# Agent attention and a tanh feed-forward: the low part of the hidden tile for two of eight pairs by DMA, and no f32 passes

## The chip, the core and the metric

One core of a Trainium2 chip. The metric is device time in microseconds of the whole program, inputs in HBM to output in HBM; three runs of the kernel before gave 2227.61, 2227.90 and 2228.77 us, median 2227.9.

## What is computed

Four batches of 12480 queries go through an attention with 49 agents in place of the keys, and the result through a feed-forward layer of width 2048 with the nonlinearity h - tanh(h):

```python
a2k = sm(agents, k)          # 49 x 12480, scale 1/sqrt(128)
agent_v = a2k @ v            # 49 x 128
q2a = sm(q, agents)          # 12480 x 49
x = q2a @ agent_v            # 12480 x 128, for each of 4 batches
h = x @ w_in                 # 128 -> 2048
g = h - np.tanh(h)
out = g @ w_out              # 2048 -> 128
```

## The kernel before

`agent_v @ w_in` is folded into one 49 x 2048 matrix per batch, kept as a high and a low part (`awh`, `awl`), so that h comes straight from the softmax weights of the queries. The program has a start (batch 0's keys and values, the weights, which arrive as 64-bit floats and are decoded), and then one long loop.

The loop runs over 104 blocks of 480 queries, and in each block over 8 **pairs** of hidden chunks (a chunk is 128 of the 2048 hidden units, so a pair tile is 128 partitions x 960 values). That makes 832 steps. One step of pair k, and the name of each piece, which the rest uses:

- **m1** (L398, L399, TensorE): four matmuls of 480 columns write h into PSUM. Three PSUM buffers hold h, so m1 of pair k+3 waits until pair k has been read.
- **y, z** (L408, L410, ScalarE): y = tanh(c h), z = y*y.
- **g** (L412, VectorE): g = h*z. The host-side factor makes this the small-h form of h - tanh(h).
- **gh** (L442, GpSimd): g rounded to the matmul's short f32 format (fp32r), the high part.
- **gl** (L447, VectorE): g - gh, the low part.
- **m2** (L459, L460, L461, TensorE): for each of the two chunks three matmuls of 480 columns into the block's accumulator: gh by the low and by the high part of w_out (`wo_l`, `wo_h`), and gl by `wo_h`. So six for a pair.

One pair in sixteen is **plain**: the last pair of every even block (`PLAIN_PAIR`, `PLAIN_EVERY`) has no gh and no gl; its g is multiplied in full f32 by `wo_f` (L457), which the hardware runs as two instructions for each chunk, four for the pair. There are 52 plain pairs and 780 others.

Beside the loop run, in pieces, the softmax of the queries two blocks ahead (L353 to L390) and, in batches 0 to 2, the next batch's keys and values (L228 to L290). Loads and stores are all issued by SyncE (SP): the queries `qt`, the keys `kt`, the values `v`, the output.

The order of the instructions on each engine is set by a scheduler when the program is built; `LAG1` and `LAG2` keep the gl and the m2 one step each behind in the text of the program. At run time each engine works through its own list in that order and waits where an operand or a free buffer is missing. The `NB` table gives the number of buffers of each tile.

Of the kernel before, what the change touches and what calls it, by code (L numbers as in the profile page):

```python
# [11 lines left out]
F32 = mybir.dt.float32  # L12
F32R = mybir.dt.float32r
# [4 lines left out]
AF = mybir.ActivationFunctionType  # L18
ALU = mybir.AluOpType
# [3 lines left out]
B, N, C = 4, 12480, 128  # L23
A = 49
A2 = 2 * A
FF = 2048
NCH = FF // 128
# [7 lines left out]
BLK = 480  # L35
# [21 lines left out]
T0 = 13  # L57
# [15 lines left out]
class Build:  # L73
# [11 lines left out]
        self.work = ctx.enter_context(self.pool(name, reuse_waits="tile"))  # L85

    def wtile(self, tag, bufs):
        return self.work.tile([128, 1024], F32, tag=tag, name=tag, bufs=bufs)

    def misc(self):  # L90
        return self.pmisc.tile([128, 512], F32, tag="misc", name="misc")
# [1 line left out]
    def constants(self):  # L93
        nc = self.nc
        c = self.const
        self.ag = c.tile([128, B, A], F32, tag="ag", name="ag")
        nc.sync.dma_start(self.ag, self.agT.rearrange("b c a -> c b a"))
        self.ident = c.tile([128, 128], F32, tag="ident", name="ident")
        make_identity(nc, self.ident)
        self.identr = c.tile([128, 128], F32R, tag="identr", name="identr")  # L100
        nc.vector.tensor_copy(self.identr, self.ident)
        self.ones = c.tile([128, 128], F32, tag="ones", name="ones")
        nc.vector.memset(self.ones, 1.0)
        self.mx = c.tile([128, NP * B], F32, tag="mx", name="mx")
# [4 lines left out]
        self.wo_f = c.tile([128, 2, C], F32, tag="wo_f", name="wo_f")  # L109
# [40 lines left out]

    def load_w_out(self, c, raw):
        nc = self.nc
        w = self.work.tile([128, 512], F32, tag="wf", name="wf", bufs=2)
        self.decode(raw, w)
        h = self.wo_h[:, 4 * c : 4 * c + 4, :].rearrange("p n e -> p (n e)")
        l = self.wo_l[:, 4 * c : 4 * c + 4, :].rearrange("p n e -> p (n e)")
        nc.scalar.copy(h, w)
        nc.vector.tensor_tensor(l, w, h.bitcast(F32), ALU.subtract)
        if c == PLAIN_PAIR // 2:
            nc.scalar.copy(self.wo_f.rearrange("p n e -> p (n e)"), w[:, 2 * C * (PLAIN_PAIR % 2) :][:, : 2 * C])  # L160

    def phase1(self, b):
        nc = self.nc
        st = {}
        kb, vb = (KV0 if b == 0 else KV), VB

# [125 lines left out]
        def sums():  # L292
            yield
            yield
            acc, an = (st["ps"] if b == 0 else st["acc"]), st["acc"]
            sm = self.small.tile([128, 1], F32, tag="sm", name="sm")
            nc.vector.tensor_scalar(sm[:A], acc[:A, C : C + 1], EPS, None, ALU.add)
            nc.vector.reciprocal(sm[:A], sm[:A])
            nc.vector.tensor_scalar(an[:A, :C], acc[:A, :C], sm[:A], None, ALU.mult)
            pt = self.misc()  # L300
            nc.tensor.transpose(pt[:, :A], an[:A, :C], self.ident[:A, :A])
# [103 lines left out]
    def act(self, h):  # L405
        nc = self.nc
        y = self.pair(self.wtile("y", NB["y"]))
        nc.scalar.activation(y, h[:, :, :BLK], AF.Tanh, scale=TSC)  # L408
        z = self.wtile("z", NB["z"])[:, : 2 * BLK]
        nc.scalar.activation(z, y.rearrange("p c n -> p (c n)"), AF.Square)  # L410
        g = self.wtile("g", NB["g"])[:, : 2 * BLK]
        nc.vector.tensor_tensor(self.pair(g), h[:, :, :BLK], self.pair(z), ALU.mult)  # L412
# [26 lines left out]

    def high(self, g):  # L440
        gh = self.wtile("gh", NB["gh"])[:, : 2 * BLK].bitcast(F32R)
        self.nc.gpsimd.tensor_scalar(gh, g, 1.0, 0.0, ALU.mult, ALU.add)  # L442
        return gh

    def low(self, g, gh):
        gl = self.wtile("gl", NB["gl"])[:, : 2 * BLK].bitcast(F32R)
        self.nc.vector.tensor_tensor(gl, g, gh.bitcast(F32), ALU.subtract)  # L447
        return gl

    def m2(self, acc, i, gh, gl):  # L450
        nc = self.nc
        for c in range(2):
            f = 2 * i + c
            x = slice(c * BLK, (c + 1) * BLK)
            first, last = f == 0, f == NCH - 1
            if gl is None:
                nc.tensor.matmul(acc[:, :BLK], self.wo_f[:, c, :], gh[:, x], start=first, stop=last)  # L457
# [3 lines left out]
            nc.tensor.matmul(acc[:, :BLK], self.wo_h[:, f, :], gl[:, x], start=False, stop=last)  # L461

    def fast(self):
        nc, tc = self.nc, self.tc
# [41 lines left out]
        rest0 = p1[2 * NG + 5 :] + [t_job(1)]  # L506
        live = []
        kq = []
        q1, q2, done = [], [], []
        acc, outs = {}, {}  # L510

        def start(gen):
# [18 lines left out]

        def rest(n, i, h):
            g = self.act(h)
            even = n % PLAIN_EVERY == 0
            plain = even and i == PLAIN_PAIR
            gh = None if plain else self.high(g)
            q1.append((n, i, g, gh))

        def low(keep):
            while len(q1) > keep:  # L540
                n, i, g, gh = q1.pop(0)
                q2.append((n, i, g, None) if gh is None else (n, i, gh, self.low(g, gh)))

        def out(keep):
            while len(q2) > keep:
                n, i, gh, gl = q2.pop(0)
                if i == 0:
                    acc[n] = self.misc()
                self.m2(acc[n], i, gh, gl)
                if i == HP - 1:  # L550
                    done.append(n)

        for n, i in steps:
            b = blocks[n][0]
            pos = (n % 2) * HP + i
            p = n // 2
            if n % NBLK == 0 and i == 0 and b + 1 < B:
                kq = self.phase1(b + 1)
            h = foreground(n, i)
# [84 lines left out]
```

## Time and profile before

| | |
|---|---|
| median of the runs | 2227.9 us |
| span of the profiled execution, first to last instruction | 2226.8 us |
| steps in the loop | 832 |
| TensorE busy | 2181.5 us |
| VectorE busy | 2044.3 us |
| ScalarE busy | 1812.7 us |
| GpSimd busy | 1410.9 us |
| moved by the SP queue | 106.68 MB |
| mean granted TensorE clock | 0.992 |

The times of single instructions come from this one execution, whose span is 1.1 us below the median of the runs. Matmuls overlap: one that is listed with 0.38 us can be followed by the next 0.22 us later, and so the time from start to start is what a matmul costs in a row of them, and the busy time says only that the engine had something under way.

### The profile page before, as it was taken

To read this page: it belongs to the slowest core of one execution; us is meant where nothing else is said; L and a number is where in the kernel's file an instruction comes from. 1 tells how busy PE (TensorE), PEld (TensorE's weight loads), DVE (VectorE), ACT (ScalarE), POOL (GpSimd) and SP (SyncE) were. 2 spreads that over 40 slices of the span, in tenths; PEclk is the share of its full clock that TensorE was granted. 3 is DMA by queue.
4 is the path that set the end of the run, shared out by engine and by line. 5 is a ranking of instruction groups with operands and counts; after the bars stand their busy time and mean duration, and the time that the engine had idled before them with its cause. 6 is when DMAs were issued, how large, how long until landed. Compare 5 with 4: busy or idle time off the path is not lost.

```text
span 2226.8 us, 31246 instructions
## 1 busy us (share of the span) xinstructions
PE 2181.5 (98%) x11083; PEld 1838.3 (83%) x11083; DVE 2044.3 (92%) x2107; ACT 1812.7 (81%) x2179; POOL 1410.9 (63%) x957
## 2 busy tenths in 40 slices
PE   7699999999999999999999999999999999999998
PEld 7588878888888887888888888788888888888887
DVE  6998998889998999888999999988999999999998
ACT  3478887778887877877888878877889989898987
POOL 2555566656765647665666555766666767676776
PEclk9899999999999999999999999999999999999999
DMA  9411111211011110211011210121010000000000
GB/s 300 120 56 56 57 37 47 65 50 35 28 46 56 56 58 30 63 56 58 19 36 38 65 55 21 37 64 49 19 36 19 28 27 28 27 27 27 27 10 20
DMA packets 76658, 108.75 MB, mean 49 GB/s; under 512 B 4048, under 2 KB 56528, under 8 KB 76496
## 3 DMA queue, kind: packets, MB, share of 16 engines
q1 hardware_dynamic: 76496, 106.68, 15.1%
q8 instruction: 91, 1.49, 0.3%
q14 instruction: 71, 0.58, 0.1%
HBM read 81.10 MB, written 25.56 MB: 48 GB/s over the span
## 4 chain that ended last, share of the span: by engine, by line
PE 90%; DVE 5%; POOL 2%; issue 1%; ACT 1%; DMA 0%; POOLq 0%; SPq 0%; ACTq 0%; DVEq 0%
PE h L398 16%; PE h L399 15%; PE misc L461 15%; PE misc L459 14%; PE misc L460 14%; PE misc L457 4%; PE misc L353 4%; PE misc L276 3%; PE misc L228 3%; DVE gl L447 1%; DVE g L412 1%; POOL gh L442 1%; PE h L209 1%; PE misc L385 1%; PE misc L327 0%
## 5 line engine op out<-in xcount | busy, mean ns | idle before, releaser
L442 POOL TENSOR_SCALAR gh<-g 128x960 fp32r<-128x960 f32 x780 | 1201.8, 1542 | 636.1 <-DVE g L412 488.9
L447 DVE TENSOR_TENSOR gl<-g,gh 128x960 fp32r<-128x960 f32 x780 | 977.6, 1254 | 88.6 <-PE misc L461 62.3
L412 DVE TENSOR_TENSOR g<-h,z 128x960 f32<-128x960 f32 x832 | 950.9, 1147 | 55.7 <-ACT z L410 53.3
L408 ACT ACTIVATE y<-h 128x960 f32<-128x960 f32 x832 | 804.2, 971 | 214.1 <-PE h L399 207.6
L410 ACT ACTIVATE z<-y 128x960 f32<-128x960 f32 x832 | 832.5, 1007 | 24.8 <-DVE g L412 7.8
L398 PE MATMUL h<-pT,awh 98*128 98x480 f32 x1664 | 666.9, 401 | 1.8 <-DVE g L412 1.3
L399 PE MATMUL h<-pT,awl 98*128 98x480 f32 x1664 | 631.6, 380 | 0.0
L461 PE MATMUL misc<-gl,wo_h 128*128 128x480 f32 x1560 | 608.7, 390 | 3.9 <-DVE gl L447 3.8
L459 PE MATMUL misc<-gh,wo_l 128*128 128x480 f32 x1560 | 594.2, 381 | 3.8 <-POOL gh L442 3.6
L460 PE MATMUL misc<-gh,wo_h 128*128 128x480 f32 x1560 | 591.2, 379 | 0.0
L398 PEld LDWEIGHTS h<-pT,awh 98*128 98x128 f32 x1664 | 312.8, 188 | 65.3 <-issue 14.0
L399 PEld LDWEIGHTS h<-pT,awl 98*128 98x128 f32 x1664 | 314.5, 189 | 58.8 <-issue 11.9
L461 PEld LDWEIGHTS misc<-gl,wo_h 128*128 128x128 f32 x1560 | 292.4, 187 | 59.1 <-DVE gl L447 8.7
L459 PEld LDWEIGHTS misc<-gh,wo_l 128*128 128x128 f32 x1560 | 294.3, 189 | 54.0 <-POOL gh L442 11.1
L460 PEld LDWEIGHTS misc<-gh,wo_h 128*128 128x128 f32 x1560 | 292.9, 188 | 47.9 <-issue 0.2
L378 POOL TENSOR_TENSOR pp<-qe,pp 120x392 fp32r<-120x392 f32 x52 | 70.6, 1357 | 67.9 <-ACT pp L376 67.6
L353 PEld LDWEIGHTS misc<-ag,qt 128*120 128x120 f32 x832 | 96.8, 187 | 3.3
L353 PE MATMUL misc<-ag,qt 128*120 128x49 f32 x832 | 94.2, 267 | 0.0
L457 PE MATMUL misc<-g,wo_f 128*128 128x480 f32 x208 | 92.6, 567 | 0.0
L366 POOL TENSOR_TENSOR qe<-qe,qm 120x392 f32<-120x392 f32 x52 | 71.0, 1366 | 30.0 <-ACT qe L364 29.9
L522 ACT ACTIVATE o<-misc 128x480 f32<-128x480 f32 x104 | 58.7, 565 | 36.4 <-PE misc L457 22.8
L276 PEld LDWEIGHTS misc<-v,ke 128*49 128x49 f32 (+1 forms) x588 | 62.0, 123 | 17.5 <-issue 12.9
(85 smaller groups left out, 993.7 us busy)
## 6 DMA issues: line engine op xcount, KB each, us to landing
qt<-qT SPq DMA_DIRECT2D x52, 480.0 KB, 3.4
outT<-o SPq DMA_DIRECT2D x52, 480.0 KB, 2.6
kt<-kT SPq DMA_DIRECT2D x48, 512.0 KB, 3.6
v<-v SPq DMA_DIRECT2D x48, 512.0 KB, 4.1
raw<-w_in SPq DMA_DIRECT2D x4, 512.0 KB, 7.8
raw<-w_out SPq DMA_DIRECT2D x4, 512.0 KB, 9.5
kt<-kT SPq DMA_DIRECT2D x4, 128.0 KB, 2.0
v<-v SPq DMA_DIRECT2D x4, 64.0 KB, 1.9
```

The source lines that it names most:

```text
L353: nc.tensor.matmul(ps[:TT, t * A : (t + 1) * A], qt[:, t * TT : (t + 1) * TT], self.ag[:, b, :], start=True, stop=True)
L398: nc.tensor.matmul(h[:, c, :BLK], aw[0][:A2, sl], pT[:A2], start=True, stop=False)
L399: nc.tensor.matmul(h[:, c, :BLK], aw[1][:A2, sl], pT[:A2], start=False, stop=True)
L408: nc.scalar.activation(y, h[:, :, :BLK], AF.Tanh, scale=TSC)
L410: nc.scalar.activation(z, y.rearrange("p c n -> p (c n)"), AF.Square)
L412: nc.vector.tensor_tensor(self.pair(g), h[:, :, :BLK], self.pair(z), ALU.mult)
L442: self.nc.gpsimd.tensor_scalar(gh, g, 1.0, 0.0, ALU.mult, ALU.add)
L447: self.nc.vector.tensor_tensor(gl, g, gh.bitcast(F32), ALU.subtract)
L457: nc.tensor.matmul(acc[:, :BLK], self.wo_f[:, c, :], gh[:, x], start=first, stop=last)
L459: nc.tensor.matmul(acc[:, :BLK], self.wo_l[:, f, :], gh[:, x], start=first, stop=False)
L460: nc.tensor.matmul(acc[:, :BLK], self.wo_h[:, f, :], gh[:, x], start=False, stop=False)
L461: nc.tensor.matmul(acc[:, :BLK], self.wo_h[:, f, :], gl[:, x], start=False, stop=last)
```

## The change

The f32 passes are gone: every pair has a gh, with `wo_f` replaced by a third copy of w_out. In two of the eight pairs of a block (i = 1 and i = 5; 208 in all) VectorE's gl is replaced by two DMAs: SP copies g into the gl tile (L455), and then a DMA on GpSimd's queue adds gh to it (L459). For the sum to be a difference, gh is made with the opposite sign of g. The signs are set by negating the folded matrix (`avs`), so that g comes out negated and gh positive, and gl is the negated low part, multiplied by the negated `wo_n`. In the text below such a pair is called a **late pair**: its four high matmuls (L468, L469) stand at its place in m2, and its two low ones (L471) behind the m2 of the next pair.

Buffers: gh 3 to 4, gl 2 to 3, the keys' tiles in the loop 3 to 2, the decode tile of w_out 2 to 1; the work tiles have 960 instead of 1024 columns.

```diff
-KV = 3
+KV = 2
-PLAIN_PAIR = NCH // 2 - 1
-PLAIN_EVERY = 2
+DMA_EVERY = 4
+DMA_AT = 1
-NB = dict(y=2, z=2, g=4, gh=3, gl=2)
+NB = dict(y=2, z=2, g=4, gh=4, gl=3)
...
-        w = self.work.tile([128, 512], F32, tag="wf", name="wf", bufs=2)
+        w = self.work.tile([128, 512], F32, tag="wf", name="wf", bufs=1)
...
-        if c == PLAIN_PAIR // 2:
-            nc.scalar.copy(self.wo_f.rearrange("p n e -> p (n e)"), w[:, 2 * C * (PLAIN_PAIR % 2) :][:, : 2 * C])
+        n = self.wo_n[:, 4 * c : 4 * c + 4, :].rearrange("p n e -> p (n e)")
+        nc.scalar.activation(n, h.bitcast(F32), AF.Copy, scale=-1.0)
...
-            nc.vector.tensor_copy(self.avs[:, b, :A], pt[:, :A])
-            nc.scalar.copy(self.avs[:, b, A:], pt[:, :A])
+            nc.vector.tensor_scalar(self.avs[:, b, :A], pt[:, :A], -1.0, None, ALU.mult)
+            nc.scalar.activation(self.avs[:, b, A:], pt[:, :A], AF.Copy, scale=-1.0)
...
-        self.nc.gpsimd.tensor_scalar(gh, g, 1.0, 0.0, ALU.mult, ALU.add)
+        self.nc.gpsimd.tensor_scalar(gh, g, -1.0, 0.0, ALU.mult, ALU.add)
...
-        self.nc.vector.tensor_tensor(gl, g, gh.bitcast(F32), ALU.subtract)
+        gl = self.low_tile()
+        self.nc.vector.tensor_tensor(gl, g, gh.bitcast(F32), ALU.add)
         return gl

-    def m2(self, acc, i, gh, gl):
+    def low_copied(self, g):
+        gl = self.low_tile()
+        self.nc.sync.dma_start(gl.bitcast(F32), g)
+        return gl
+
+    def low_added(self, gl, gh):
+        self.nc.gpsimd.dma_start(gl.bitcast(F32), gh.bitcast(F32), accum_op=ALU.add)
+        return gl
+
+    def m2(self, acc, i, gh, gl, high=True, low=True):
...
-            if gl is None:
-                nc.tensor.matmul(acc[:, :BLK], self.wo_f[:, c, :], gh[:, x], start=first, stop=last)
-                continue
-            nc.tensor.matmul(acc[:, :BLK], self.wo_l[:, f, :], gh[:, x], start=first, stop=False)
-            nc.tensor.matmul(acc[:, :BLK], self.wo_h[:, f, :], gh[:, x], start=False, stop=False)
-            nc.tensor.matmul(acc[:, :BLK], self.wo_h[:, f, :], gl[:, x], start=False, stop=last)
+            if high:
+                nc.tensor.matmul(acc[:, :BLK], self.wo_l[:, f, :], gh[:, x], start=f == 0, stop=False)
+                nc.tensor.matmul(acc[:, :BLK], self.wo_h[:, f, :], gh[:, x], start=False, stop=False)
+            if low:
+                nc.tensor.matmul(acc[:, :BLK], self.wo_n[:, f, :], gl[:, x], start=False, stop=f == NCH - 1)
...
-            gh = None if plain else self.high(g)
-            q1.append((n, i, g, gh))
+            gh = self.high(g)
+            q1.append((n, i, g, gh, self.low_copied(g) if i % DMA_EVERY == DMA_AT else None))
...
-                self.m2(acc[n], i, gh, gl)
+                self.m2(acc[n], i, gh, gl, low=not late)
+                while q3:
+                    self.m2(*q3.pop(0), high=False)
+                if late:
+                    q3.append((acc[n], i, gh, gl))
```

Three places in the order that the scheduler made.

On TensorE the plain pair is gone. Before, at the end of an even block (names carry the tile's buffer number; h is the result of m1, gh and gl are the operands of m2, misc is the accumulator):

```order
L461 MATMUL misc_20133<-gl_20258,wo_h_84 128x480
L457 MATMUL misc_20133<-g_20256,wo_f_86 128x480 x2
L398 MATMUL h_20333<-pT_20150,awh_15307 128x480
L399 MATMUL h_20333<-pT_20150,awl_15308 128x480
L398 MATMUL h_20333<-pT_20150,awh_15307 128x480
L399 MATMUL h_20333<-pT_20150,awl_15308 128x480
```

In the change every pair has its six rows, as the next excerpt shows for gl_19698. It is again TensorE, around the low matmuls of one late pair, whose high part is gh_19651 and whose low part is gl_19653:

```order
L468 MATMUL misc_19570<-gh_19651,wo_l_85 128x480
L469 MATMUL misc_19570<-gh_19651,wo_h_84 128x480
L398 MATMUL h_19756<-pT_19587,awh_15741 128x480
L399 MATMUL h_19756<-pT_19587,awl_15742 128x480
L398 MATMUL h_19756<-pT_19587,awh_15741 128x480
L399 MATMUL h_19756<-pT_19587,awl_15742 128x480
L468 MATMUL misc_19570<-gh_19675,wo_l_85 128x480
L469 MATMUL misc_19570<-gh_19675,wo_h_84 128x480
L471 MATMUL misc_19570<-gl_19698,wo_n_86 128x480
L468 MATMUL misc_19570<-gh_19675,wo_l_85 128x480
L469 MATMUL misc_19570<-gh_19675,wo_h_84 128x480
L471 MATMUL misc_19570<-gl_19698,wo_n_86 128x480
L471 MATMUL misc_19570<-gl_19653,wo_n_86 128x480 x2
```

The high matmuls of the late pair stand first, then m1 of the fifth pair after it (h_19756), then the whole m2 of the next pair, and only then the two low ones.

On GpSimd, two late pairs (gh_19651, and gh_19744, which comes four pairs later):

```order
L442 TENSOR_SCALAR gh_19651<-g_19649 128x960
L459 DMA gl_19653<-gh_19651 128x960
L366 TENSOR_TENSOR qe_19641<-qe_19641,qm_19640 120x392
L442 TENSOR_SCALAR gh_19675<-g_19673 128x960
L442 TENSOR_SCALAR gh_19696<-g_19694 128x960
L442 TENSOR_SCALAR gh_19719<-g_19717 128x960
L442 TENSOR_SCALAR gh_19744<-g_19742 128x960
L442 TENSOR_SCALAR gh_19770<-g_19768 128x960
L378 TENSOR_TENSOR pp_19736<-qe_19641,pp_19736 120x8x49
L459 DMA gl_19746<-gh_19744 128x960
```

The adding DMA stands right behind its gh, or, as for the second one and for most of the 208, behind the gh of the next pair.

More of the change, by code (lines that the diff above doesn't have):

```diff
@@ L87, in wtile @@
     def wtile(self, tag, bufs):
-        return self.work.tile([128, 1024], F32, tag=tag, name=tag, bufs=bufs)
+        return self.work.tile([128, 2 * BLK], F32, tag=tag, name=tag, bufs=bufs)
     def misc(self):
@@ L508, in fast @@
         kq = []
-        q1, q2, done = [], [], []
+        q1, q2, q3, done = [], [], [], []
         acc, outs = {}, {}
@@ L533, in rest @@
             g = self.act(h)
-            even = n % PLAIN_EVERY == 0
-            plain = even and i == PLAIN_PAIR
-            gh = None if plain else self.high(g)
-            q1.append((n, i, g, gh))
+            gh = self.high(g)
+            q1.append((n, i, g, gh, self.low_copied(g) if i % DMA_EVERY == DMA_AT else None))
         def low(keep):
             while len(q1) > keep:
-                n, i, g, gh = q1.pop(0)
-                q2.append((n, i, g, None) if gh is None else (n, i, gh, self.low(g, gh)))
+                n, i, g, gh, gl = q1.pop(0)
+                late = gl is not None
+                q2.append((n, i, gh, self.low_added(gl, gh) if late else self.low(g, gh), late))
         def out(keep):
             while len(q2) > keep:
-                n, i, gh, gl = q2.pop(0)
+                n, i, gh, gl, late = q2.pop(0)
                 if i == 0:
                     acc[n] = self.misc()
-                self.m2(acc[n], i, gh, gl)
+                self.m2(acc[n], i, gh, gl, low=not late)
[3 more added lines that the diff above has]
+                    q3.append((acc[n], i, gh, gl))
                 if i == HP - 1:
```

6 lines of the change are left out of this document (3 added, 3 removed).

## The prediction

> **What bounds the kernel now.** I read the page first: the busy times and the chain of work that ended last.
>
> ```profile
> span 2226.8 us, 31246 instructions
> PE 2181.5 (98%) x11083; PEld 1838.3 (83%) x11083; DVE 2044.3 (92%) x2107; ACT 1812.7 (81%) x2179; POOL 1410.9 (63%) x957
> PE 90%; DVE 5%; POOL 2%; issue 1%; ACT 1%; DMA 0%; POOLq 0%; SPq 0%; ACTq 0%; DVEq 0%
> ```
>
> TensorE (PE) carries 90% of the chain. The busy times by stage say where the rest is.
>
> ```profile
> 60.00:120.00 60.00, 40.41 (x215) 31.63 (x214) 55.05 (x70) 31.61 (x45) 31.91 (x25) 0.83 0.34 100
> 700.00:1200.00 500.00, 497.79 (x2520) 416.96 (x2519) 459.49 (x469) 413.06 (x493) 316.27 (x216) 1.00 0.15 47
> 1700.00:2150.00 450.00, 450.00 (x2177) 380.59 (x2176) 433.34 (x431) 404.62 (x466) 322.53 (x204) 1.00 0.08 26
> ```
>
> Columns: stretch, its length, busy time of PE, PE's weight loads, DVE, ACT, POOL, granted clock, DMA share, GB/s. Before 120 us VectorE leads, with 55 of 60 us, and PE waits. In the loop PE is busy in 497.8 of 500 and then in 450 of 450 us at full clock. A busy PE could still hide gaps, so I read the timeline around one plain pair, PE alone.
>
> ```profile
> 1902.57 0.38 PE L461 MATMUL misc<-gl,wo_h 128*128 128x480 f32 x1
> 1902.79 1.77 PE L457 MATMUL misc<-g,wo_f 128*128 128x480 f32 x4
> 1904.02 0.76 PE L398 MATMUL h<-pT,awh 98*128 98x480 f32 x1
> 1904.62 0.38 PE L399 MATMUL h<-pT,awl 98*128 98x480 f32 x1
> 1904.84 0.38 PE L398 MATMUL h<-pT,awh 98*128 98x480 f32 x1
> ...
> 1909.09 0.39 PE L461 MATMUL misc<-gl,wo_h 128*128 128x480 f32 x1
> 1917.83 0.39 PE L461 MATMUL misc<-gl,wo_h 128*128 128x480 f32 x1
> ```
>
> Between the last two rows 40 matmuls start in 8.74 us, 0.2185 us each and without a hole. So the loop is bound by the number of PE passes: fewer passes shorten it, and an operand that comes late lengthens it by all its lateness. VectorE, at 92%, is next.
>
> **The f32 passes.** The chain in order of time gives the plain pair's place on PE:
>
> ```profile
> 1902.95 1.61 PE misc L457 x4
> 1940.63 1.61 PE misc L457 x4
> ```
>
> 1.61 us, once in 37.68 us (two blocks). In its place come six matmuls, 6 x 0.2185 = 1.31 us. The gain is 0.30 us, times 52: **-15.5 us**, on the path, since PE never waits here. This is all that PE can gain, as all other matmuls keep their number.
>
> **What VectorE and GpSimd get.** The groups by line:
>
> ```profile
> L442 POOL TENSOR_SCALAR gh<-g 128x960 fp32r<-128x960 f32 x780 | 1201.8, 1542 | 636.1 <-DVE g L412 488.9
> L447 DVE TENSOR_TENSOR gl<-g,gh 128x960 fp32r<-128x960 f32 x780 | 977.6, 1254 | 88.6 <-PE misc L461 62.3
> L412 DVE TENSOR_TENSOR g<-h,z 128x960 f32<-128x960 f32 x832 | 950.9, 1147 | 55.7 <-ACT z L410 53.3
> L408 ACT ACTIVATE y<-h 128x960 f32<-128x960 f32 x832 | 804.2, 971 | 214.1 <-PE h L399 207.6
> L410 ACT ACTIVATE z<-y 128x960 f32<-128x960 f32 x832 | 832.5, 1007 | 24.8 <-DVE g L412 7.8
> ```
>
> VectorE loses 780 - 624 = 156 gl, 156 x 1.254 = 196 us. It lies beside a full PE and shortens nothing; it brings slack. GpSimd gains 52 gh, 52 x 1.542 = 80 us, also hidden while its list stays under PE's: in two blocks 16 x 1.54 us of gh and two softmax pieces (2 x 1.36 us) make 27.4 of 37.4 us, and 10 us are left for four adding DMAs.
>
> **The late pair: does its low part come in time?** This decides. After g of a late pair k: SP copies g, GpSimd waits for the copy to land and for gh, issues the adding DMA, and PE needs the sum at its two low matmuls. Nothing like the adding DMA is in the trace of before. First the time that is there. One pair in the loop:
>
> ```profile
> 1905.48 0.97 ACT L408 ACTIVATE y<-h 128x960 f32<-128x960 f32 x1 [0.31 <-PE h L399]
> 1906.48 1.01 ACT L410 ACTIVATE z<-y 128x960 f32<-128x960 f32 x1
> 1906.59 1.94 DVE L447 TENSOR_TENSOR gl<-g,gh 128x960 fp32r<-128x960 f32 x1 [0.76 <-POOL gh L442]
> 1908.45 1.14 DVE L412 TENSOR_TENSOR g<-h,z 128x960 f32<-128x960 f32 x1
> 1909.77 1.75 POOL L442 TENSOR_SCALAR gh<-g 128x960 fp32r<-128x960 f32 x1 [2.25 <-DVE g L412]
> 1910.58 1.14 DVE L412 TENSOR_TENSOR g<-h,z 128x960 f32<-128x960 f32 x1
> 1911.65 1.14 DVE L447 TENSOR_TENSOR gl<-g,gh 128x960 fp32r<-128x960 f32 x1
> 1911.90 1.76 POOL L442 TENSOR_SCALAR gh<-g 128x960 fp32r<-128x960 f32 x1 [0.38 <-DVE g L412]
> ```
>
> Its m1 starts at 1904.02, its g ends at 1909.59: 5.6 us, of which 1.0 is g standing behind a gl. The least is 4 x 0.22 + 0.97 + 1.01 + 1.14 = 4.0. With a quarter of the gl gone I take 5.2.
>
> The order of the change then says how much PE work stands between a late pair's m1 and its low matmuls. For gl_19653 it is 54 matmuls of 480 columns (11.8 us) and eight small f32 ones with four transposes (1.7 us by the rows of the softmax): 13.5 us, less 5.2 leaves 8.3 us from the end of g. Counted so for all late pairs, the cover runs from 7.2 to 11.9 us; about half have over 9.
>
> Then the time that is needed. The adding DMA mostly stands behind the gh of the next pair, which ends at 1913.66, 4.1 us after the first g's end at 1909.59. The copy has landed by then, by the DMA issues:
>
> ```profile
> qt<-qT SPq DMA_DIRECT2D x52, 480.0 KB, 3.4
> outT<-o SPq DMA_DIRECT2D x52, 480.0 KB, 2.6
> kt<-kT SPq DMA_DIRECT2D x48, 512.0 KB, 3.6
> q1 hardware_dynamic: 76496, 106.68, 15.1%
> ```
>
> 480 KB land 2.6 to 3.4 us after issue, less than 4.1. From issue to landing of the adding DMA (call it X) lies between 2.6 us, the quickest row of the same size, and 6.8 us, twice the slowest, as it must read both operands and write one. With no better row I take the nearest, the load at **3.4 us**. The need is 4.1 + 3.4 = 7.5 us. Where cover is short of the need, PE waits the difference; the late pair four on had its m1 before that wait and keeps the time as cover. Summed so over the 208 late pairs, PE loses 4 us at a need of 7.5, 13 at 8.0, 31 at 8.5, 55 at 9.0, 91 at 9.5, and 217 at 10.9 (X of 6.8). I take **+4 us**; the lower end (X of 2.6, need 6.7) is nothing.
>
> The Trainium skill (DMA: Bandwidth & Descriptors, section "Anatomy of one DMA — SWDGE (gpsimd) path") gives a DMA from GpSimd's queue 2.0 us plus its bytes at 436 GB/s, an estimate of 3.1 us for 480 KB, by which the need were 7.2 and the loss about nothing; it is for plain DMAs, and no run here shows one from that queue yet.
>
> What else hangs on the sum: g(k+5) on VectorE stands behind a gl that reuses the late pair's gl buffer, and the fourth gh after it reuses its gh. Both come after the low matmuls or some 9 us after g, so they only hurt if the need passes about 9.5.
>
> **The rest.** Traffic: 208 copies and 208 additions of 480 KB add 204 MB to 106.68, and half as much again for the second read; at the same rate per byte 15.1% becomes about 58%, so the queues have room. The keys' buffers go from three to two; SP waits for them now:
>
> ```profile
> SPq L177 <- PE misc L228: 293.2, 36, 13.4
> ```
>
> In the new order a load still stands 16 us or more of PE work ahead of its use against 3.6 us to land: nothing. At the start the decode of w_out has one buffer where two followed closely:
>
> ```profile
> 70.70 1.50 POOL L135 TENSOR_TENSOR wf<-rem,de 128x512 f32<-128x512 f32 x1 [0.63 <-DVE rem L134]
> 72.83 1.64 POOL L135 TENSOR_TENSOR wf<-rem,de 128x512 f32<-128x512 f32 x1 [0.63 <-DVE rem L134]
> 76.70 0.68 DVE L158 TENSOR_TENSOR wo_l<-wf,wo_h 128x512 fp32r<-128x512 f32 x1
> 82.26 0.31 PE L301 MATMUL misc<-ident,acc 49*128 49x49 f32 x1 [15.03 <-DVE acc L299]
> ```
>
> The second decode now waits for the L158 at 76.70, some 4 us; but PE waits for L299, which moves ahead of about 2 us of decode work on VectorE. Four extra ScalarE negations of some 0.6 us lie beside. I take 0, with 3 us either way.
>
> **Sum.** Span 2226.8 - 15.5 + 4 = 2215.3; the median of the runs lies 1.1 above the span: **2216 us**.
>
> **The rivals.** (1) *The low part is late.* The same place, with X above 4.0: at a need of 8.1 the waits eat the 15.5 us, and beyond it the kernel is slower. X of 5.1, half above the load's 3.4, gives 9.2, about +70: 2282. For it: the addition moves three streams, GpSimd must first make the descriptors, and copies share the queues with loads. Against it: VectorE's slack brings g earlier than 5.2. (2) *GpSimd becomes the bound.* It waits in its list for the copy. If each addition holds it for over 2.5 us, 27.4 + 4 x 2.5 passes PE's 37.4; at 3.5 us it is 4 us more in two blocks, 52 times: about 2420. Against it: most additions stand behind a further gh, when the copy has landed. (3) *It cancels*: a need of 8.0 to 8.4, 2224 to 2232.
>
> The Trainium skill (SBUF — State Buffer, section "Who interferes with whom") says that a VectorE instruction with two SBUF inputs blocks a GpSimd one that reads SBUF; the trace agrees, as the gh of 1.75 us above lies beside a gl. By it gh shortens where a gl is gone, which would lower the need by up to 0.75 us, an estimate from the page's rule and the shortest gh of about 1.0 us.
>
> **Chances.** Forecast, hidden but for a few us (2206 to 2223): 0.47. Late (1): 0.35. GpSimd (2): 0.07. Cancels (3): 0.11. What a measurement can tell from no change is 0.2%, 4.5 us. Faster 0.47, same 0.11, slower 0.42. The range goes from 2206 (all hidden, a better start) to 2285 (a need of 9.25), leaving out rival 2 and the far end of rival 1, some 0.18. The forecast's own range is 2206 to 2223.
>
> **What would show it.** Right: L457 gone, L471's idle time under some 10 us, L459's landing near 3.4 us, VectorE near 1850 us. Wrong: idle PE ahead of L471 that is put down to the DMA of gl (rival 1); gh late, with GpSimd waiting for the copy and PE for gh (rival 2). A landing above 4 us makes the forecast wrong.

## The result, and the profile after

The changed kernel takes **2327.1 us** (median of four runs, 2320.0 to 2336.9) against 2228.3 us, a ratio of **1.0447 with a 95% interval of 1.042 to 1.0474**: 99 us slower. The forecast was 2216 us, and the time lies outside its range of 2206 to 2285. The profiled execution took 2336.9 us, span 2335.1, and was the slowest of the four; shares and waits below are of that one. Two executions of a slower state, in which TensorE's granted clock was low throughout (one of experiment 1, 3034 us at 0.651, and one of the kernel before beside it, 2392 us at 0.846), are left out of the ratios.

The page of the changed kernel: busy times, the chain that ended last, groups by line, and the DMA issues (last column: us from issue to landing).

```profile
span 2335.1 us, 32593 instructions
PE 2228.6 (95%) x11187; PEld 1870.9 (80%) x11187; DVE 1917.0 (82%) x1951; ACT 1789.0 (77%) x2182; POOL 1449.0 (62%) x1217
PE 66%; DMA 15%; DVE 8%; issue 5%; POOL 4%; ACT 2%; SPq 0%; POOLq 0%; DVEq 0%; ACTq 0%
...
L442 POOL TENSOR_SCALAR gh<-g 128x960 fp32r<-128x960 f32 x832 | 1109.7, 1347 | 634.7 <-DVE g L412 455.1
L450 DVE TENSOR_TENSOR gl<-g,gh 128x960 fp32r<-128x960 f32 x624 | 814.6, 1307 | 146.7 <-POOL gh L442 98.7
L459 POOL DMA_DIRECT2D gl<-gh x208 | 184.3, 886 | 139.4 <-DMA gl<-g 42.1
...
gl<-g SPq DMA_DIRECT2D x208, 480.0 KB, 2.8
gl<-gh POOLq DMA_DIRECT2D x208, 480.0 KB, 4.4
```

TensorE carried 90% of the chain before and carries 66% now; 15% of the chain is DMA, which was 0%. VectorE did get its relief (92% to 82%), but the kernel is no longer a full PE. The adding DMA lands 4.4 us after its issue, where the forecast took 3.4. The copy lands in 2.8 us, within the 2.6 to 3.4 us of the rows of its size before.

The waits of the changed kernel (engine, line and who ended the wait; total us, times, longest). PEld is the weight load ahead of a matmul; one wait can appear for the load and for the matmul, so the two are not added.

```profile
DVE gl L450 <- POOL gh L442: 98.7, 111, 4.5
PEld misc L471 <- DMA gl<-gh: 87.9, 86, 3.4
PE misc L471 <- DMA gl<-gh: 55.1, 51, 3.0
POOL gl L459 <- DMA gl<-g: 42.1, 25, 5.5
PEld misc L471 <- DVE gl L450: 20.8, 43, 1.9
```

In the kernel before, the first of these rows was:

```profile
DVE gl L447 <- POOL gh L442: 22.3, 44, 1.2
```

There are two kinds of wait. The late low matmuls (L471) wait for the sum. And GpSimd (POOL) waits for the copy before it can issue the addition, VectorE's gl wait for gh behind it (98.7 us in place of 22.3), and PE for gl. Counted from start to start of the matmuls, with 0.218 us for one of 480 columns, PE lost about 69 us ahead of late low matmuls (91 of them) and some 16 us ahead of others after the 120 us of the start.

One piece of the chain shows the whole path of one late pair (start us, duration, what):

```profile
1758.20 3.45 DMA gl<-g
1761.65 0.02 issue
1761.67 0.04 POOLq L459
1761.72 0.48 issue
1762.20 0.02 POOLq L442
1762.21 4.39 DMA gl<-gh
1766.60 0.04 issue
1766.65 0.71 PE misc L471 x2
```

From the end of g (the copy starts at once) to the end of the sum: 3.45 + 0.56 + 4.39 = 8.40 us, against 7.5 in the forecast. Here the addition waits for the copy, and not, as the forecast had it, for the next gh; so it is in 65 of the 198 late pairs after 200 us. Over these 198 pairs the time from the end of g to the end of the sum is 8.9 us in the mean: 4.2 to the issue, 4.7 more to the landing.

The busy times by stage, as in the prediction (length, then PE, its weight loads, DVE, ACT, POOL, clock, DMA share, GB/s):

```profile
700.00:1200.00 500.00, 481.71 (x2419) 404.72 (x2419) 405.05 (x410) 381.63 (x463) 312.30 (x259) 0.98 0.50 134
1700.00:2150.00 450.00, 434.37 (x2055) 359.60 (x2054) 386.70 (x378) 368.07 (x439) 280.77 (x245) 0.99 0.46 122
```

PE had 497.8 and 450.0 there, and 2520 and 2177 matmuls in the time; now 2419 and 2055, although a block has more of them. No engine is busy all the time; each waits for another. The clock column shows something that the forecast had not: it is no longer 1.00 in the loop.

### The profile page after: what moved, and what is told of

Its sections match the earlier page's. It is cut to its first block, busy times and chain, and to the rows that moved or that the text cites. A ratio compares the mean times of both kernels' runs of the same rounds, so it can differ in the third digit from the quotient of the medians.

```text
span 2335.1 us, 32593 instructions
## 1 busy us (share of the span) xinstructions
PE 2228.6 (95%) x11187; PEld 1870.9 (80%) x11187; DVE 1917.0 (82%) x1951; ACT 1789.0 (77%) x2182; POOL 1449.0 (62%) x1217
## 4 chain that ended last, share of the span: by engine, by line
PE 66%; DMA 15%; DVE 8%; issue 5%; POOL 4%; ACT 2%; SPq 0%; POOLq 0%; DVEq 0%; ACTq 0%
PE misc L471 13%; DMA gl<-gh 11%; PE h L398 11%; PE misc L468 11%; PE misc L469 11%; PE h L399 11%; DMA gl<-g 4%; PE misc L353 3%; DVE g L412 3%; POOL gh L442 3%; PE misc L228 2%; DVE gl L450 2%; PE misc L276 2%; PE h L209 1%; ACT y L408 1%
## 5 line engine op out<-in xcount | busy, mean ns | idle before, releaser
L442 POOL TENSOR_SCALAR gh<-g 128x960 fp32r<-128x960 f32 x832 | 1109.7, 1347 | 634.7 <-DVE g L412 455.1
L450 DVE TENSOR_TENSOR gl<-g,gh 128x960 fp32r<-128x960 f32 x624 | 814.6, 1307 | 146.7 <-POOL gh L442 98.7
L471 PE MATMUL misc<-gl,wo_n 128*128 128x480 f32 x1664 | 622.8, 400 | 64.5 <-DMA gl<-gh 55.1
L468 PE MATMUL misc<-gh,wo_l 128*128 128x480 f32 x1664 | 643.7, 387 | 4.2 <-POOL gh L442 4.1
L469 PE MATMUL misc<-gh,wo_h 128*128 128x480 f32 x1664 | 635.7, 382 | 0.0
L471 PEld LDWEIGHTS misc<-gl,wo_n 128*128 128x128 f32 x1664 | 306.9, 190 | 155.5 <-DMA gl<-gh 87.9
L398 PEld LDWEIGHTS h<-pT,awh 98*128 98x128 f32 x1664 | 315.7, 190 | 72.9 <-DVE g L412 15.5
L468 PEld LDWEIGHTS misc<-gh,wo_l 128*128 128x128 f32 x1664 | 317.0, 190 | 55.9 <-POOL gh L442 9.6
L469 PEld LDWEIGHTS misc<-gh,wo_h 128*128 128x128 f32 x1664 | 316.7, 190 | 48.5
L459 POOL DMA_DIRECT2D gl<-gh x208 | 184.3, 886 | 139.4 <-DMA gl<-g 42.1
L228 PEld LDWEIGHTS misc<-ag,kt 128*128 128x128 f32 x588 | 81.4, 207 | 3.8
L276 PE MATMUL misc<-v,ke 128*49 128x129 f32 (+1 forms) x588 | 79.5, 281 | 0.0
```

The costliest lines, as they stand in the source:

```text
L276: nc.tensor.matmul(ps[:A, : C + 1], e3[:r, t, :], vt[:r, t, : C + 1], start=(first and t == 0), stop=(last and t == n - 1),)
L398: nc.tensor.matmul(h[:, c, :BLK], aw[0][:A2, sl], pT[:A2], start=True, stop=False)
L442: self.nc.gpsimd.tensor_scalar(gh, g, -1.0, 0.0, ALU.mult, ALU.add)
L450: self.nc.vector.tensor_tensor(gl, g, gh.bitcast(F32), ALU.add)
L471: nc.tensor.matmul(acc[:, :BLK], self.wo_n[:, f, :], gl[:, x], start=False, stop=f == NCH - 1)
```

## The experiments

All times are medians. Every run stood beside runs of the kernel before on the same chip (2228.2 to 2228.6 us). Edits are against the changed kernel unless said. The scheduler lays each kernel's lists anew, so that an edit can also move instructions that it doesn't name; differences of a few us between variants are not read for that reason. The variants `e1_read_gh`, `e4_no_add`, `e9_no_copy`, `e10_sync_queue`, `e11_half_add` and `e15_copy_only` do not put the whole low part of the late pairs into the output; the others compute everything.

**1. PE no longer waits for the sum** (`e1_read_gh`).

```diff
-                    q3.append((acc[n], i, gh, gl))
+                    q3.append((acc[n], i, gh, gh))
```

> The two low matmuls of a late pair read its negated high part in place of the sum (its low part is left out of the output); copy, adding DMA, GpSimd's list and the number of PE passes stay as in the changed kernel, only PE's wait for the sum is gone. Theory A (PE loses its time waiting for the landing of the sum, and through the clock that falls after the long waits): nearly all of the loss goes, 2212 to 2222 us, no half-clock stretch in the loop. Rival B (the adding DMA holds GpSimd's list, so that gh, VectorE's gl and later g are late by themselves): PE still waits for plain gl and gh, 2240 us or more. Rival C (the added traffic slows everything): about 2300 us.

Measured: **2267.9 us**, ratio 1.0178 (1.0158 to 1.0199). 59 us of the 99 go, 40 stay. That is outside theory A's range and in rival B's (2240 us or more), whose waits are there too; but more than half of the loss was PE's wait for the sum. The busy times by stage tell where the rest stays:

```profile
700.00:1200.00 500.00, 497.76 (x2558) 423.52 (x2557) 433.37 (x435) 409.57 (x496) 342.77 (x277) 1.00 0.52 141
1700.00:2150.00 450.00, 426.60 (x2013) 352.52 (x2012) 394.38 (x362) 359.69 (x426) 282.75 (x241) 0.98 0.45 120
```

In the middle PE is full again, with 2558 matmuls in place of the changed kernel's 2419. In the last quarter, without the keys' and values' work on PE (a step of the kernel before takes 2.35 us there and 2.61 in the middle), it is far from full. The timeline there, one place that comes back every two blocks:

```profile
1785.78 1.80 POOL L442 TENSOR_SCALAR gh<-g 128x960 fp32r<-128x960 f32 x1 [2.32 <-DVE qs L372]
1789.02 0.89 POOL L459 DMA_DIRECT2D gl<-gh  x1 [1.44 <-DMA gl<-g]
1789.65 1.30 POOL L442 TENSOR_SCALAR gh<-g 128x960 fp32r<-128x960 f32 x1
1790.62 1.25 POOL L378 TENSOR_TENSOR pp<-qe,pp 120x392 fp32r<-120x392 f32 x1
1791.28 4.58 DVE L450 TENSOR_TENSOR gl<-g,gh 128x960 fp32r<-128x960 f32 x2
1791.55 2.22 POOL L442 TENSOR_SCALAR gh<-g 128x960 fp32r<-128x960 f32 x2
...
1794.84 0.48 PE L471 MATMUL misc<-gl,wo_n 128*128 128x480 f32 x1 [1.97 <-DVE gl L450]
```

GpSimd stands 1.44 us at the copy, then issues; its next gh, a softmax piece and two more gh follow close on each other; VectorE's gl come late and PE waits 1.97 us for one. Here the late matmuls also hold gh longer than in the changed kernel, so the 40 us are not GpSimd's list alone.

**2. The low matmuls at a later place** (`e2_later_low`), and **its buffers without it** (`e5_buffers_only`).

```diff
-NB = dict(y=2, z=2, g=4, gh=4, gl=3)
+NB = dict(y=2, z=2, g=4, gh=4, gl=4)
...
-                self.m2(acc[n], i, gh, gl, low=not late)
-                while q3:
-                    self.m2(*q3.pop(0), high=False)
+                mid = bool(q3) and i % DMA_EVERY == (DMA_AT + 2) % DMA_EVERY
+                self.m2(acc[n], i, gh, gl, low=not late and not mid)
+                if mid:
+                    self.m2(*q3.pop(0), high=False)
+                    self.m2(acc[n], i, gh, gl, high=False)
```

(Both variants have one buffer instead of two for the output tile, to make room.)

> The low matmuls of a late pair move behind the next pair's step and the high part of the pair after it, 8 or more matmuls of 0.2185 us later (1.75 us more cover), with a fourth gl buffer, for which the output has one buffer less. Theory A: the need of about 8.9 us from the end of g is met for most late pairs, 2212 to 2232 us. Rival B (GpSimd's list held up): at most half of the loss goes, 2270 us or more.

> The changed kernel with the buffers of the run with later low matmuls (four for gl, one for the output) and nothing else. If there the later place brought the 59 us, this stays at 2310 to 2335 us; if the fourth gl buffer did, it comes to 2260 to 2285 us.

Measured: **2268.0 us**, 1.0177 (1.0159 to 1.0196), with the later place; **2334.2 us**, 1.048 (1.0463 to 1.0498), with the buffers alone. So the later place, an estimated 1.75 us more cover, is worth 66 us, and the buffers alone gain nothing, as their first expectation had it. The later place misses theory A's range and ends just under rival B's 2270: waits for the sum have fallen from 69 to about 25 us by the same count, and about 40 us of the loss are left. (They are as many as in experiment 1, but not the same ones: there PE has no wait for the sum at all.)

**3. The two halves of the change, one at a time**: no DMA, all low parts on VectorE (`e3_all_vector`), and DMA low parts with the f32 pairs kept (`e12_f32_kept`).

```diff
-            q1.append((n, i, g, gh, self.low_copied(g) if i % DMA_EVERY == DMA_AT else None))
+            q1.append((n, i, g, gh, self.low_copied(g) if False else None))
```

```diff
+            if gl is None:
+                nc.tensor.matmul(acc[:, :BLK], self.wo_f[:, c, :], gh[:, x], start=f == 0, stop=f == NCH - 1)
+                continue
...
-            gh = self.high(g)
+            gh = None if n % 2 == 0 and i == HP - 1 else self.high(g)
```

(`wo_f` is made again at the start, from the negated weights.)

> No copies and no adding DMAs: VectorE makes the low part of all 832 pairs, f32 passes gone. If the term of -15.5 us is right and VectorE (1917 + 208 x 1.3 = about 2190 us busy of 2212) still keeps up: 2210 to 2220 us. If VectorE becomes the bound: 2225 us or more, with PE waiting for gl and g.

> The changed kernel with its DMA low parts, but the 52 f32 pairs kept (the first buffers are 12 instead of 13 to make room). If the two halves of the change add up (21 us with the f32 passes gone and no DMA, the rest by the late sums): about 2306 us. If the pair that needs no gh and no gl gives VectorE and GpSimd the time to catch up after a late sum: 2260 to 2295 us. If it only costs PE its 15.5 us: about 2340 us.

Measured: **2249.5 us**, 1.0096 (1.0079 to 1.0113), with no DMA; **2282.6 us**, 1.0246 (1.0229 to 1.0263), with the f32 pairs kept. The first stands against the forecast's surest term: without the f32 passes and with nothing late, the kernel is 21 us slower, not 15.5 faster. Its last stage:

```profile
1700.00:2150.00 450.00, 444.85 (x2141) 370.12 (x2141) 449.58 (x432) 396.05 (x453) 330.17 (x210) 1.00 0.08 26
```

VectorE is busy 449.6 of 450 us (433.3 before): it has no time left there. (GpSimd's list counts too; see experiment 7.) The second says that the halves do not add up (21 + 54 = 75, not 99): beside late sums it is worth 44 us to keep the pair without gh and gl. It fell within the expectation that this pair is time in which VectorE and GpSimd catch up; but up to 32 of the 44 us can be TensorE's clock (last section), which has no half-speed stretch in the loop of `e12_f32_kept`.

**4. The price of the addition**: the same DMA as a plain write (`e4_no_add`), and the addition of half the columns (`e11_half_add`, run once).

```diff
-        self.nc.gpsimd.dma_start(gl.bitcast(F32), gh.bitcast(F32), accum_op=ALU.add)
+        self.nc.gpsimd.dma_start(gl.bitcast(F32), gh.bitcast(F32))
```

```diff
-        self.nc.gpsimd.dma_start(gl.bitcast(F32), gh.bitcast(F32), accum_op=ALU.add)
+        self.nc.gpsimd.dma_start(gl[:, :BLK].bitcast(F32), gh[:, :BLK].bitcast(F32), accum_op=ALU.add)
```

> The DMA on GpSimd's queue stays, but writes the negated high part plainly over the copy instead of adding it (the low part of late pairs is left out of the output). If the addition (a second operand read, and the sum written) makes the 4.4 us from issue to landing, it falls to 2.8 to 3.4 us, as for loads of that size, and the time to 2225 to 2275 us. If GpSimd's queue itself makes it, it stays at 4.0 us or above and the time within 2300 to 2335 us.

> The adding DMA takes only the first 480 of 960 columns (the second half of the low part of late pairs is left out); one look, for its time from issue to landing, 4.4 us for 480 KB. If that is set by bytes: 2.2 to 3 us; if it is mostly a fixed time: 3.5 to 4.2 us.

Measured: **2255.0 us**, 1.0125 (1.0108 to 1.0142), and 2300.9 us in a single execution of the second. The DMA issues of the plain write, then of the half addition:

```profile
gl<-gh POOLq DMA_DIRECT2D x208, 480.0 KB, 2.9
```

```profile
gl<-gh POOLq DMA_DIRECT2D x208, 240.0 KB, 3.2
```

The first fell within its expectation for the addition as the cause. A plain write from GpSimd's queue lands in 2.9 us, the addition in 4.4: the addition itself costs 1.5 us. GpSimd also spends longer on its issue, 886 ns against 591. Together they cost 72 us of the program (2327.1 - 2255.0). Half the bytes land in 3.2 us, so by these two points an addition is 2.0 us and 1.2 us for each 240 KB. The expectation for the half (3.5 to 4.2, or 2.2 to 3) missed on both sides: neither bytes alone nor a mostly fixed time.

**5. Fewer late pairs**: only in even blocks (`e6_even_blocks`), the same at the later place (`e7_even_later`), and one in two blocks at the later place (`e8_once_later`).

```diff
-            q1.append((n, i, g, gh, self.low_copied(g) if i % DMA_EVERY == DMA_AT else None))
+            q1.append((n, i, g, gh, self.low_copied(g) if n % 2 == 0 and i % DMA_EVERY == DMA_AT else None))
```

(`e8_once_later` has `n % 2 == 0 and i == 5` there; the later place is the edit of experiment 2.)

> Late pairs only in the even blocks, 104 of 208; the odd blocks, where most pieces of the query softmax stand on ScalarE and VectorE, make all low parts on VectorE. Theory A2 (the sum is late above all where the softmax makes g late: 55 of 69 us of the waits before late low matmuls were in odd blocks): 2225 to 2240 us, with some 15 us of such waits. Rival (each late pair costs the same): half the loss, about 2270 us. Rival V (VectorE, with 728 low parts, holds PE up in the odd blocks, as it did with all 832 on it): 2240 to 2255 us with PE waiting for plain gl and gh.

> The same 104 late pairs with the later place of their low matmuls and four gl buffers. Theory A2: waits for the sum are gone, 2212 to 2222 us, faster than before. Rival V: 2230 us or more, with waits for plain gl and gh.

> One late pair in two blocks (the sixth pair of each even block), 52 in all, low matmuls at the later place: VectorE makes 780 low parts as before the change, the f32 passes are gone, GpSimd has 52 gh and 52 adding DMAs more. If fewer passes are worth 15.5 us as soon as VectorE has no more than before: 2212 to 2222 us. If the f32 pair was also placed where VectorE needs the relief (two pairs ahead of the softmax): 2225 to 2240 us.

Measured: **2258.5 us**, 1.0141 (1.0124 to 1.0158); **2240.4 us**, 1.0053 (1.0036 to 1.007); **2255.8 us**, 1.0118 (1.0101 to 1.0135). None of the three first ranges held. `e6_even_blocks` came out between rival V's 2240 to 2255 and the 2270 of the other rival, and `e8_once_later` above both of its ranges; only rival V's bound for `e7_even_later` (2230 us or more, with waits for plain gl and gh) held. In that one the waits for the sum are down to 10.4 us by the row of L471's weight loads (87.9 in the changed kernel); what is left is this:

```profile
DVE gl L450 <- POOL gh L442: 114.3, 132, 1.8
POOL gl L459 <- DMA gl<-g: 31.8, 31, 2.4
PEld misc L468 <- POOL gh L442: 28.1, 61, 0.9
```

PE and VectorE wait for GpSimd's gh. And `e8_once_later` is slower than the kernel before although VectorE has as many low parts as there: the number of them does not decide alone.

**6. GpSimd's queue**: a plain write from GpSimd with no copy (`e9_no_copy`), the same write from SP (`e10_sync_queue`), and no DMA from GpSimd at all, PE reading the copy of g (`e15_copy_only`).

```diff
-        self.nc.sync.dma_start(gl.bitcast(F32), g)
...
-        self.nc.gpsimd.dma_start(gl.bitcast(F32), gh.bitcast(F32), accum_op=ALU.add)
+        self.nc.gpsimd.dma_start(gl.bitcast(F32), gh.bitcast(F32))
```

```diff
-        self.nc.sync.dma_start(gl.bitcast(F32), g)
...
-        self.nc.gpsimd.dma_start(gl.bitcast(F32), gh.bitcast(F32), accum_op=ALU.add)
+        self.nc.sync.dma_start(gl.bitcast(F32), gh.bitcast(F32))
```

```diff
-        self.nc.gpsimd.dma_start(gl.bitcast(F32), gh.bitcast(F32), accum_op=ALU.add)
```

> As the run without addition (a plain write on GpSimd's queue, 2255 us), and the copies on SP's queue are left out too (the low part of late pairs is left out of the output). GpSimd then never waits in its list for a copy, and half of the added traffic is gone; the order of GpSimd's list and its 208 issues stay. Theory L (the rest of the loss comes from GpSimd standing at the copy, and from the copies' share of the queues): 2215 to 2235 us. Rival V (the rest is there without any DMA, as the 21 us with all low parts on VectorE): 2250 us or more.

> As the run before it, but the plain write is issued on SP's queue, so that GpSimd's list holds only gh and the softmax pieces and VectorE has 624 low parts. If the -15.5 us of the f32 passes are there as soon as VectorE and GpSimd keep up: 2210 to 2218 us. If the issues on GpSimd's queue cost nothing: the same as the run before it. If it stays above 2230 us, the term itself is wrong.

> The changed kernel without the adding DMA: PE's low matmuls of a late pair read the copy of g (that leaves the subtraction of the high part out of the output). GpSimd issues no DMA, the copies stay. If the copies cost nothing by themselves: 2215 to 2230 us, as with the plain write on SP's queue (2228 us). If their traffic, or g being held until the copy has read it, matters: 2240 us or more.

Measured: **2269.7 us**, 1.0183 (1.0166 to 1.02); **2227.9 us**, 0.9998 (0.9989 to 1.0008); **2210.9 us**, 0.9923 (0.9906 to 0.994). The first came out above rival V's bound, but not for rival V's reason, as the second shows: their edits differ in the issuing queue alone, and their times by 42 us. Without the copy the scheduler puts the write directly behind its own gh in GpSimd's list, where GpSimd also waits for PE's low matmuls, which free gl's buffer. The profile books these waits at the gh next to the write; with the write on GpSimd's queue, then on SP's:

```profile
POOL gh L442 <- PE misc L470: 117.5, 54, 3.8
POOL gh L442 <- PE misc L470: 13.2, 13, 2.6
```

So the 42 us are for what the list waits for as well as for the 0.6 us that an issue takes, and they hold for this order of the list, which is not that of the changed kernel. The second lies above its first range (2210 to 2218) and below the 2230 that would have made the term of the f32 passes wrong. The third came out below its range of 2215 to 2230. It is the kernel of the forecast without the addition. Its busy times, its stages, and PE's largest waits for gl and gh:

```profile
PE 2165.7 (98%) x11187; PEld 1857.0 (84%) x11187; DVE 1871.6 (85%) x1951; ACT 1784.5 (81%) x2182; POOL 1354.4 (61%) x1009
```

```profile
700.00:1200.00 500.00, 497.80 (x2560) 423.87 (x2560) 425.47 (x433) 407.19 (x496) 302.29 (x229) 1.00 0.27 93
1700.00:2150.00 450.00, 450.00 (x2225) 390.00 (x2224) 397.07 (x403) 399.78 (x473) 312.80 (x218) 1.00 0.20 77
```

```profile
PEld misc L470 <- DVE gl L450: 9.5, 19, 1.1
PEld misc L467 <- POOL gh L442: 4.7, 15, 0.8
```

PE is full in both stages, 17.3 us are gained, and 208 copies of 480 KB through SP cost nothing that shows. Everything that was lost, 2327.1 - 2210.9 = 116 us, comes with the adding DMA. Why the write on SP's queue is still 17 us behind the copy alone was not separated; there gh is held until a DMA has read it, in the copy-only kernel it is not, and the load of weights ahead of L467 waits 29.2 us for gh there, 4.7 here.

**7. Other hands for the 52 pairs that were f32 pairs**: their high part on ScalarE, with the late pairs of `e7_even_later` (`e13_later_scalar`) and without any DMA (`e14_all_vector_scalar`); then also a low part on GpSimd (`e16_low_on_gpsimd`, `e17_one_scalar`).

```diff
+        if scalar:
+            self.nc.scalar.activation(gh, g, AF.Copy, scale=-1.0)
+            return gh
...
-            gh = self.high(g)
+            gh = self.high(g, n % 2 == 0 and i == HP - 1)
```

(`e16_low_on_gpsimd` has `i >= HP - 2` there. Both of the last two have `(self.nc.gpsimd if pool else self.nc.vector).tensor_tensor(...)` in `low`, with `pool` for the last pair of even blocks.)

> As the run with late pairs in the even blocks and later low matmuls (2240 us), with the high part of the 52 pairs that were f32 pairs made by ScalarE instead of GpSimd. If GpSimd's longer list (52 gh more than before, and the adding DMAs) is what is left of the loss: 2215 to 2230 us. If ScalarE or VectorE cannot take it, or the loss lies elsewhere: 2238 us or more.

> As the run with no DMA and all low parts on VectorE (2249 us), with the high part of the 52 pairs that were f32 pairs made by ScalarE. If GpSimd's 52 gh more are what PE waits for there: 2215 to 2232 us. If VectorE with its 52 low parts more is the bound: 2244 us or more.

> No DMA low parts. In each even block ScalarE makes the high parts of the last two pairs, and GpSimd makes the low part of the last one, so that VectorE has 780 low parts as before the change and GpSimd 728 high and 52 low parts; four gl buffers, one output buffer. If it is enough that VectorE and GpSimd have no more than before: 2210 to 2222 us, faster than both kernels. If the low part on GpSimd (longer than a high part) or the high parts on ScalarE make PE wait: 2230 us or more.

> As the run before it, with ScalarE making only the high part of the last pair of each even block. If ScalarE's second high part costs more than it relieves: faster than the run before it, 2210 to 2225 us. If GpSimd's list is what counts: slower than it by 5 us or more.

Measured: **2242.8 us**, 1.0067 (1.005 to 1.0084); **2238.8 us**, 1.005 (1.0033 to 1.0066); **2251.9 us**, 1.0101 (1.0084 to 1.0118); **2246.2 us**, 1.0078 (1.0061 to 1.0094). Without DMAs, taking 52 gh off GpSimd is worth 11 us of the 33 between experiment 3 and the forecast, which lies between the two expectations; beside the late pairs it is worth nothing, as the second expectation (ScalarE or VectorE cannot take it, or the loss lies elsewhere) had it. A low part on GpSimd makes it worse, as its second expectation had it: there GpSimd stands and waits for ScalarE's gh, 160 us in the first of the two and 104 in the second. With one gh on ScalarE instead of two it is 6 us faster, but not down to the 2210 to 2225 expected.

No run that computes everything came under the kernel before.

## Why the prediction was wrong, step by step

The term that failed is the +4 us for the late pair's sum. With all that it sets off the adding DMA cost 116 us, as its landing took 4.4 us in place of 3.4, and as the step that called the longer list of GpSimd hidden beside a full PE did not hold. The other term, -15.5 us, is there in the copy-only kernel.

- **What bounds the kernel: half right.** PE was full, and `e15_copy_only` shows that fewer passes then shorten it. But the step "VectorE loses 156 gl ... it lies beside a full PE and shortens nothing" took VectorE's and GpSimd's room for free. The row with 433.3 of 450 us busy was in front of it. The f32 pair asked nothing of either engine but a g, once in two blocks; with that gone and no DMA VectorE is at 449.6 of 450.
- **The f32 passes, -15.5 us: right, under a condition.** Measured -17.3 us in the copy-only kernel, some 0.34 us for each pair by the steps in the loop against 0.30. The condition is that VectorE has 624 low parts, that GpSimd issues nothing and, as far as `e10_sync_queue` tells, that no DMA holds gh: it meets the first two and gains nothing (2227.9).
- **The landing X, 3.4 us: the mis-sized term.** It measured 4.4 us (median; 4.3 to 7.2), a mean of 4.7. The forecast said that a landing above 4 us makes it wrong; so it was. The nearest row was a load, and a load was the wrong relative: a plain write from GpSimd's queue takes 2.9 us (experiment 4), and the rest is the addition, the one part that no row showed. The Trainium skill (DMA: Bandwidth & Descriptors, section "Anatomy of one DMA — SWDGE (gpsimd) path"), at 2.0 us plus bytes at 436 GB/s, gave an estimate of 3.1 us; the plain writes agree (2.9 and 3.1 us), and so do the 2.0 us of fixed time by the two sizes of addition, but the addition moved its bytes at half that speed.
- **m1 to the end of g, 5.2 us "with a quarter of the gl gone": wrong sign.** In the mean of the same 198 pairs it is 5.4 us before, 5.7 in the copy-only kernel and 6.2 in the changed one. VectorE had less to do, but its list stood at gl waiting for gh (98.7 us against 22.3; its idle time ahead of gl, whoever ended it, is 146.7 us against 88.6), which stood behind the addition in GpSimd's list; that this is what makes g later is a reading, and the 5.7 us without any addition show that it is not the whole. At the measured need of 8.9 us the forecast's own table gives about 50 us, and with the other 1.0 us (9.9) about 127 on the line between its last two points; PE's waits for the sum were 69. The Trainium skill's rule on VectorE and GpSimd (SBUF — State Buffer, section "Who interferes with whom") agrees in the length of gh, 1542 before and 1347 ns now (1577 with all 832 low parts on VectorE, experiment 3), but the need did not fall by it: the next pair's gh still ended 4.1 us after g in the mean. Where softmax pieces stand, in odd blocks, g was latest, and there lay 55 of the 69 us of waits.
- **GpSimd, 27.4 of 37.4 us "hidden": wrong.** The sum of an engine's work was compared with its time, where the order in its list decided: the rival "GpSimd becomes the bound" had 0.07 and a condition of over 2.5 us for each addition; by the row of L459 it was (184.3 + 139.4) / 208 = 1.6 us with its waits, and still PE and VectorE waited for its gh. It did not need to be full, only late at the places where gh is wanted next. What its list alone cost in the changed kernel is not separated: the two runs near to it give 57 us (experiment 1 against copy-only, with gh held longer as well) and 42 us (experiment 6, in another order of the list).
- **The rival "the low part is late"** had the mechanism and 0.35, with 2282 us at an X of 5.1. The measured X alone, at the need of 8.5 that follows from 4.1 + 4.4, would have given 2243 (31 us in place of 4). The feedback through g, GpSimd's list and the clock, all seen above, are left for the rest; their shares were not measured. (The rival "it cancels" has 2232 at a need of 8.4; by the forecast's own table that is about 2240.)
- **Keys' buffers, the start: right.** The first step of the third block starts 1.3 us earlier than before, within the 3 us given, and the copy-only kernel, with the same two keys' buffers, has PE full in the stage with the keys' work.

The 116 us of the adding DMA divide, by two runs, into 59 for PE's wait for the sum (2327.1 to 2267.9) and 57 for the rest (2267.9 to 2210.9): GpSimd's list, with gh held by the DMA. The second part is not divided further; GpSimd's own waits for an addition to release gh are 13.4 us (9 times) in the changed kernel. By another run (experiment 4) the 116 divide into 72 for the addition over a plain write and 44 for the write on GpSimd's queue.

## What to carry to other kernels

An engine beside a full one has no free time that its busy share tells: look at what stands behind the new instruction in its list, and who waits for that, before it is called hidden. When a term rests on an operation that no row shows, the nearest row is not its price; here an addition that lands 1.5 us later than a plain write, taken 208 times, was with its longer issue 72 of the 116 us. A pass that looks wasteful on the bounding engine can be the pause in which two others catch up.

## What was not expected of the hardware

TensorE's clock falls after waits that are short. The windows around one wait of the changed kernel (2.5 us lost ahead of L471 at 1343.80, 2.7 from start to start; the clock is the third column from the right):

```profile
1338.00:1341.70 3.70, 3.48 (x16) 2.64 (x15) 2.97 (x5) 1.91 (x2) 2.40 (x3) 1.00 0.96 243
1341.70:1345.10 3.40, 1.30 (x6) 1.15 (x7) 1.91 (x3) 2.32 (x3) 1.42 (x2) 1.00 0.12 23
1345.10:1351.90 6.80, 6.80 (x27) 6.16 (x25) 3.01 (x4) 2.92 (x4) 3.14 (x3) 0.50 0.60 143
```

PE works again at 1343.80, but the clock is 0.50 from 1345.1 to 1351.9, and a matmul of 480 columns then starts every 0.40 instead of 0.22 us. The changed kernel has 11 such stretches in the loop, 65 us in all, in steps of 3.4 us; the kernel before has none in the loop until its last microseconds. At full clock they would have been at most 32 us shorter. All waits ahead of L471 that lost 2.07 to 3.15 us were followed by one, those of 1.6 to 1.8 us only in part.

By this trace the length of the wait alone does not tell whether the clock falls; how much PE did in a fixed stretch of 3.41 us tells more. All 11 falls lie on one grid of that step. In the stretch of the grid that ends at the fall PE was busy for 29 to 58% of the time, and for 52% or less in 10 of the 11; no stretch of the loop from 60% up was followed by a fall. Three stretches of the grid:

```profile
1505.54:1508.95 3.41, 0.98 (x5) 0.86 (x6) 2.07 (x2) 1.51 (x2) 1.00 (x1) 1.00 0.35 74
1300.74:1304.15 3.41, 1.77 (x11) 1.21 (x10) 3.30 (x4) 1.92 (x3) 2.89 (x2) 1.00 0.77 144
2167.72:2171.14 3.42, 2.19 (x10) 1.53 (x9) 2.04 (x2) 3.13 (x5) 2.62 (x2) 1.00 0.52 95
```

After the first two the clock fell, after the third it did not. The last two hold waits of the same length, 1.8 us lost ahead of 1303.79 and of 2171.54; but the second of these runs over the border at 2171.14 and is shared by two stretches.

The border is not sharp: in experiments 1 and 2 stretches of 49 and 56% kept the clock and one of 65% lost it. The Trainium skill (TensorE: Matmul & The Clock Gate, section "Part 1: The HAM clock gate (the "warmup" mystery)") has the clock fall after an idle window of about 3.4 us; the steps agree, but here a part of a window was enough.
